# Two linear-attention blocks and two MLP blocks on one core, rewritten on a dependency graph whose order a list scheduler settles

## The chip, the cores and the metric

The kernel runs on one core of a Trainium2 chip, as one launch. The metric is the device time of one execution in microseconds (us), lower being better. Five engines work side by side, each through its own list of instructions in order: TensorE (PE in the profile; PEld is its weight load), VectorE (DVE), ScalarE (ACT), GpSimd (POOL) and SyncE (SP), which here issues DMAs only. They meet through semaphores. PSUM, where matmuls end, has eight banks of 128 x 512 fp32.

## The reference

x has 2048 rows of 512. Four layers follow each other, A, B, A, B, with the same weights both times; each takes a layernorm of x and adds its result to x.

```python
def _A_ref(x, wqkv, wo):                       # called with _layernorm(x); H = 32 heads of 16
    qkv = (x @ wqkv).reshape(B, S, 3, H, Dh)   # -> q, k, v
    phi = lambda t: jnp.where(t > 0, t + 1, jnp.exp(t)) + 1e-6
    pq, pk = phi(q), phi(k)
    kv = jnp.einsum("bhsd,bhse->bhde", pk, v)
    z = jnp.einsum("bhsd->bhd", pk)
    num = jnp.einsum("bhqd,bhde->bhqe", pq, kv)
    den = jnp.einsum("bhqd,bhd->bhq", pq, z)[..., None] + 1e-6
    return (num / den).reshape(B, S, D) @ wo

def _B_ref(x, w1, b1, w2, b2):                 # called with _layernorm(x); F = 1792
    y = _layernorm(x)
    h = gelu_tanh(y @ w1 + b1)
    return h @ w2 + b2
```

kv and z sum over all 2048 rows, so the second half of a layer A can't begin before its first half has ended. Every other step is by rows.

## The kernel before

The rows are cut into 16 tiles of 128 and 4 chunks of 4 tiles. Python writes the order out by hand: each layer is a generator that emits, step by step, the stages of several tiles, each stage some steps behind the one before (A_LAGS, AB_LAGS, B_LAGS). x stays in SBUF as fp32 (`xsb`).

Layer A, first half, by tile: the layernorm (`ln_stats`, L316 to L323: stats, their aggregate and veps on DVE, a power of -1/2 on POOL; L383: the normalized tile in bf16 on DVE), a DMA transpose from the SP queue into `yTA` (L368), then q as 16 matmuls of 128 columns (L429), k (L439) and v (L447) as 4 of 512 each. phi is exp and relu on ACT (L461 to L465), then a minimum and an addition on DVE (L481 to L499). v is copied out of PSUM, in half the tiles by DVE (L472) and in the others by ACT. Per tile 4 matmuls of 128 columns (L515) add to K'V and 4 of 8 columns (L518) to z. At the end DVE masks both to the heads' diagonal blocks (`KVm` L560, `Zm` L562).

Second half, by tile: numerator (L576) and denominator (L578) as 4 matmuls each, the numerator copied to SBUF by ACT (L595), the reciprocal on DVE (L602, L617), the product on POOL (L618), a transpose by 4 matmuls (L645) with its copy by ACT (L649), wo (L668) and the addition to x on DVE (L677).

Layer B, by chunk: the same layernorm, with the normalized tile on ACT (L379), a DMA transpose into `yTB`, w1 in 14 groups of 4 matmuls of 512 columns (L764). The gelu takes five passes over each 128 x 512 group, half of the groups with ACT's square and half with DVE's: ACT L784 and L788, DVE L804, L814, L822, L826, ACT's sigmoid L837, DVE's product L851. w2 is 14 matmuls by tile (L865) and a fifteenth for b2 (L867); L873 adds to x.

A layer's matmuls wait until the layer before has issued all of its own: `prev_pe_done` and `my_pe_done` hold them back, while layernorms may run ahead. At the start SP loads x in four parts of 512 KB, the first of which ACT turns to fp32 (L272); POOL loads wqkv, wo, w1 and w2, one DMA each. At the end ACT makes bf16 of each tile (L1000) and SP stores it.

## Time and profile before

| | before |
|---|---|
| three timed runs | 418.62, 419.04, 420.08 us; median 419.04 |
| span of the profiled execution | 415.4 us, 6985 instructions |
| busy PE, DVE, ACT, POOL | 364.7, 309.6, 316.6, 76.5 us |
| mean granted TensorE clock | 0.978 |

The profiled execution is known by its span, from its first to its last instruction: 415.4 us. The timed runs show 3.6 us more in the median for what lies around the span. A busy time adds up instructions that may overlap (matmuls are pipelined, and the next elementwise instruction starts some 0.1 us before the one ahead has ended), so it is above the time that the engine needs. The granted clock is a share of full speed; TensorE has two levels, 1.2 and 2.4 GHz.

### The profile page before, as it was taken

To read this page: it belongs to the slowest core of one execution; us is meant where nothing else is said; L and a number is where in the kernel's file an instruction comes from. 1 tells how busy PE (TensorE), PEld (TensorE's weight loads), DVE (VectorE), ACT (ScalarE), POOL (GpSimd) and SP (SyncE) were. 2 spreads that over 40 slices of the span, in tenths; PEclk is the share of its full clock that TensorE was granted. 3 is DMA by queue.
4 is the path that set the end of the run, shared out by engine and by line. 5 is a ranking of instruction groups with operands and counts; after the bars stand their busy time and mean duration, and the time that the engine had idled before them with its cause. 6 is when DMAs were issued, how large, how long until landed. Compare 5 with 4: busy or idle time off the path is not lost.

```text
span 415.4 us, 6985 instructions
## 1 busy us (share of the span) xinstructions
PE 364.7 (88%) x2465; PEld 185.4 (45%) x2465; DVE 309.6 (75%) x868; ACT 316.6 (76%) x563; POOL 76.5 (18%) x115
## 2 busy tenths in 40 slices
PE   0869997979967999999999999796996799999986
PEld 0546665544422444445435666553432244444432
...
DMA packets 40448, 18.80 MB, mean 45 GB/s; under 512 B 35229, under 2 KB 39326, under 8 KB 40414
## 3 DMA queue, kind: packets, MB, share of 16 engines
...
## 4 chain that ended last, share of the span: by engine, by line
PE 62%; DVE 19%; ACT 8%; DMA 5%; issue 4%; POOL 1%; ACTq 0%; POOLq 0%
PE ps L865 24%; PE ps L764 19%; PE ps L429 5%; PE ps L439 4%; DVE stats L316 4%; DMA yTA<-ybuf 4%; PE ps L447 4%; DVE xsb L677 3%; ACT ub L784 3%; ACT sgb L837 2%; PE ps L867 2%; PE ps L668 2%; DVE rr L617 2%; DVE mv L317 1%; DVE ybuf L383 1%
## 5 line engine op out<-in xcount | busy, mean ns | idle before, releaser
L764 PE MATMUL ps<-yTB,w 128*128 128x512 bf16 x448 | 103.8, 380 | 9.9 <-ACT qb L788 7.9
L865 PE MATMUL ps<-w,bigB 128*128 128x512 bf16 x448 | 102.1, 379 | 5.5 <-DVE bigB L851 5.5
L784 ACT ACTIVATE ub<-ps,b1c 128x512 bf16<-128x512 f32 x112 | 78.4, 704 | 19.5 <-DVE bigB L851 14.2
L323 POOL TENSOR_TENSOR rstd<-veps,neghalf 128x1 f32<-128x1 f32 x64 | 36.4, 568 | 219.3 <-DVE veps L322 148.3
L837 ACT ACTIVATE sgb<-wb 128x512 bf16<-128x512 bf16 x112 | 72.8, 653 | 3.7 <-DVE wb L822 1.9
L764 PEld LDWEIGHTS ps<-yTB,w 128*128 128x128 bf16 x448 | 40.6, 98 | 68.0 <-ACT qb L788 10.4
L865 PEld LDWEIGHTS ps<-w,bigB 128*128 128x128 bf16 x448 | 42.8, 98 | 58.9 <-DVE bigB L851 7.3
L873 DVE TENSOR_TENSOR xsb<-ps,xsb 128x512 f32<-128x512 f32 x32 | 22.0, 689 | 49.4 <-PE ps L867 49.4
L851 DVE TENSOR_TENSOR bigB<-ub,sgb 128x512 bf16<-128x512 bf16 x112 | 46.8, 419 | 12.2 <-ACT sgb L837 10.9
L316 DVE BATCH_NORM_STATS2 stats<-xsb 128x6 f32<-128x512 f32 x64 | 43.0, 671 | 8.5 <-ACT xsb L272 8.5
L461 ACT ACTIVATE ebq<-ps 128x512 bf16<-128x512 f32 x32 | 19.1, 598 | 38.6 <-PE ps L429 30.3
L429 PE MATMUL ps<-yTA,wqkv 128*128 128x128 bf16 x512 | 35.4, 224 | 12.2 <-DMA yTA<-ybuf 12.2
L618 POOL TENSOR_TENSOR ob<-numb,rr 128x512 bf16<-128x512 f32 x32 | 33.6, 1057 | 38.5 <-DVE rd L602 23.6
L788 ACT ACTIVATE qb<-ps,b1csa 128x512 bf16<-128x512 f32 x56 | 39.5, 706 | 0.0
L822 DVE SCALAR_TENSOR_TENSOR wb<-qb,ub 128x512 bf16<-128x512 bf16 x56 | 38.3, 684 | 0.0
L429 PEld LDWEIGHTS ps<-yTA,wqkv 128*128 128x128 bf16 x512 | 30.6, 100 | 13.7 <-DMA yTA<-ybuf 12.6
L668 PE MATMUL ps<-wo,oT 128*128 128x512 bf16 x128 | 35.0, 401 | 1.6 <-DVE xsb L677 1.6
L439 PE MATMUL ps<-wqkv,yTA 128*128 128x512 bf16 x128 | 34.4, 393 | 0.0
L447 PE MATMUL ps<-wqkv,yTA 128*128 128x512 bf16 x128 | 32.9, 379 | 0.0
L649 ACT ACTIVATE oT<-ps 128x512 bf16<-128x512 bf16 x32 | 19.1, 596 | 14.5 <-PE ps L645 14.4
L804 DVE TENSOR_TENSOR qb<-ub 128x512 bf16<-128x512 bf16 x56 | 23.4, 418 | 4.2 <-ACT ub L784 4.1
L379 ACT ACTIVATE ybuf<-xsb,nmr,rstd 128x512 bf16<-128x512 f32 x32 | 26.2, 819 | 0.0
...
## 6 DMA issues: line engine op xcount, KB each, us to landing
...
yTA<-ybuf SPq DMA_TRANSPOSE x32, 2.5
...
yTB<-ybuf SPq DMA_TRANSPOSE x32, 2.5
b1rows<-in_B_b_dram SPq DMA_DIRECT2D x1, 3.5 KB
```

The costliest lines, as they stand in the source:

```text
L316: t1 = dve.emit(lambda e: e.bn_stats(stats[:, ss, :], src_ap), deps=[x_dep, war_get(("stat", ss))])
L429: ins = e.matmul(ps[:, QBK[qs], kt * P:(kt + 1) * P], lhsT=wqkv_sb[:, dt, kt * P:(kt + 1) * P], rhs=yTA[:, dt, yts * P:(yts + 1) * P], sta ...
L439: ins = e.matmul(ps[:, KBK[qs], :], lhsT=yTA[:, dt, yts * P:(yts + 1) * P], rhs=wqkv_sb[:, dt, D:2 * D], start=(dt == 0), stop=(dt == DT - 1))
L447: ins = e.matmul(ps[:, VBK[qs], :], lhsT=yTA[:, dt, yts * P:(yts + 1) * P], rhs=wqkv_sb[:, dt, 2 * D:3 * D], start=(dt == 0), stop=(dt == ...
L668: ins = e.matmul(ps[:, WOBK[ws], :], lhsT=oT[:, j, ots * P:(ots + 1) * P], rhs=wo_sb[:, j, :], start=(j == 0), stop=(j == DT - 1))
L764: ins = e.matmul(ps[:, hb, :], lhsT=w1_sb[:, dt, ft * P:(ft + 1) * P], rhs=yTB[:, dt, y0 * P:(y0 + 4) * P], start=(dt == 0), stop=(dt == D ...
L784: d["t_u"] = act.emit(lambda e: e.activation(ub[:, us, :], ps[:, hb, :], ACT.Identity, bias=b1c[:, ft:ft + 1], scale=1.0), deps=[d["t_h"], ...
L788: d["t_q2"] = act.emit(lambda e: e.activation(q2b[:, us, :], ps[:, hb, :], ACT.Square, bias=b1csa[:, ft:ft + 1], scale=sa), deps=[d["t_h"] ...
L822: d["t_w"] = dve.emit(lambda e: e.scalar_tensor_tensor(out=wb[:, us, :], in0=q2b[:, us, :], scalar=1.0, in1=ub[:, us, :], op0=ALU.add, op1 ...
L837: d["t_s"] = act.emit(lambda e: e.activation(sgb[:, us, :], wb[:, us, :], ACT.Sigmoid, scale=GELU_2C), deps=[d["t_w"], war_get(("sgb", us))])
L851: t_g = dve.emit(lambda e: e.tensor_tensor(gT[:, gs, ft, :], ub[:, us, :], sgb[:, us, :], op=ALU.mult), deps=[d["t_s"], war_get(("gT", gs, ...
L865: e.matmul(ps[:, 3 + ws, :], lhsT=gT[:, gs, ft, k * P:(k + 1) * P], rhs=w2_sb[:, ft, :], start=(ft == 0), stop=False)
```

## The change

The file is written anew. Each operation is a node (`Op`) with a planned duration, the buffers that it reads and writes, and a priority; `Scheduler.run` plays the plan through and fixes each engine's order, the buffers' slots and the PSUM banks; `assign_waits` then makes the semaphore waits from the graph. In the plan each issuing queue (SP, ACT, POOL) has a transfer time of its own. At run time the lists are fixed, as before.

In the computation: v is no longer formed. Per tile y^T phi(k) is summed (`attn_g_held`: 4 matmuls of 512 columns into four PSUM banks, layer 0; `attn_g_chunk`: by chunk, added up in SBUF by DVE, layer 1), and once per layer multiplied with Wv (`attn_kv`, 16 matmuls of 128 columns). z is summed elementwise on POOL (`zacc`), and four matmuls of one column sum it over partitions. q is formed by chunk with 512 columns. Numerator and denominator are one matmul of 136 columns, times 4. DVE multiplies straight out of PSUM. The transpose ahead of wo is a DMA transpose from SP. The gelu is one ACT instruction from PSUM. b2 is added to x on POOL. x comes into bf16 tiles that the first layernorm reads directly, the last addition writes bf16. Normalized tiles of layer 0's first half are on DVE, later ones on ACT for every second tile.

The order of layers by chunk is new: `attn_out` and the MLP of chunk c, and the first half of the second layer A for that chunk, have priorities 40 us apart by chunk, so they interleave.

```diff
-                        ins = e.matmul(ps[:, VBK[qs], :], lhsT=yTA[:, dt, yts * P:(yts + 1) * P],
-                                       rhs=wqkv_sb[:, dt, 2 * D:3 * D], start=(dt == 0), stop=(dt == DT - 1))
...
+        def attn_g_held(L, st, k, y, ykey, pk, gb, prio):
+            def fn(e):
+                for dc in range(DT):
+                    ins = e.matmul(ps[:, gb.slot + dc, :], lhsT=yb[:, y.slot, dc * P:(dc + 1) * P], rhs=pkb[:, pk.slot, :],
+                                   start=(st == 0), stop=(st == ST - 1))
...
+                G.op("pool", lambda e: e.tensor_tensor(zacc[:], zacc[:], pkb[:, pk.slot, :], op=ALU.add), 1060,
...
+                    ins = e.matmul(v[:, kt, 0:136], lhsT=yTa(pq)[:, kt, k * P:(k + 1) * P],
+                                   rhs=kvz[:, kt_.slot, kt * 136:(kt + 1) * 136], start=True, stop=True)
...
+            def mul(e):
+                return e.tensor_tensor(ob[:, o.slot, :].rearrange("p (k h x) -> p k h x", k=DT, h=8),
+                                       pair(b)[:, :, 0:P].rearrange("p k (h x) -> p k h x", h=8),
+                                       rr[:, r.slot, :].rearrange("p (k h) -> p k h", k=DT).unsqueeze(3).broadcast_to([P, DT, 8, DH]),
+                                       op=ALU.mult)
+            G.op("dve", mul, 680, reads=[f"rr{L}_{st}", f"n{L}_{st}"], writes=[f"o{L}_{st}"], tiles=[b, r, o], prio=prio,
+                 name=f"o{L}_{st}", lat=40)
+            dma("sp", lambda e: e.dma_start_transpose(oT[:, ot.slot, :].rearrange("p (d s) -> p d s", d=DT), ob[:, o.slot, :]),
...
-                    d["t_s"] = act.emit(lambda e: e.activation(sgb[:, us, :], wb[:, us, :], ACT.Sigmoid, scale=GELU_2C),
...
+                G.op("act", lambda e, ft=ft, b=b: e.activation(gT[:, g.slot, ft * 512:(ft + 1) * 512], bank(b), ACT.Gelu_apprx_tanh,
+                                                               bias=b1c[:, ft:ft + 1], scale=1.0),
...
+            G.op("pool", lambda e: e.tensor_tensor(xsb[:, st, :], xsb[:, st, :], b2b[:], op=ALU.add), 1060,
...
+            busy = 1300.0 if transpose else 100.0 + kb * 1024 / 230.0
...
+                begin = max(at + 100.0, dma_free[e])
+                dma_free[e] = begin + o.nbytes
...
+                dma("act", lambda e: e.dma_start(wqkv[:, :, D:2 * D], wsrc[:, :, D:2 * D]), ["wk"], prio=-99.5, name="wk", kb=512)
+        for c in range(1, NC):
+            dma("act", lambda e, c=c: e.dma_start(
...
+                if st == 3:
+                    late("wv", "wv", wqkv[:, :, 2 * D:3 * D], wsrc[:, :, 2 * D:3 * D], pr, 512, [tr])
+                if st == 4:
+                    late("wo", "wo", wo[:], A_wo.rearrange("(dt p) c -> p dt c", p=P), pr, 512, [tr])
+                if st == 5:
+                    consts(pr, [tr])
+                if st in (6, 8):
+                    h = (st - 6) // 2
+                    late(f"w1_{h}", f"w1_{h}", w1[:, 2 * h:2 * h + 2, :], B_w1.rearrange("(dt p) c -> p dt c", p=P)[:, 2 * h:2 * h + 2, :],
+                         pr, 896, [tr])
...
+    P_A2=-30.0, P_W1=0.0, P_W2=54.0, P_K=77.0, P_G=90.0, P_Q=140.0, STEP=4.2,
+    A1_Q=58.7, A1_STEP=1.0, N_H=3, N_N=2, GAP=17.0, TABLE_PENALTY=16.9, WINDOW=199.0,
```

What this makes of the instructions is shown at three places, before and after. The first is POOL in the first half of the first layer A. Before, its list holds the power of each tile (L323) and the weights' loads (L281, L240, L243), and nothing else waits:

```order
L281 DMA wqkv<-in_A_wqkv_dram 128x4x1536
L323 TENSOR_TENSOR rstd<-veps,neghalf 128x1 [waits g_dve] x2
L240 DMA wo<-in_A_wo_dram 128x4x512
L323 TENSOR_TENSOR rstd<-veps,neghalf 128x1 [waits g_dve] x2
L251 MEMSET onesm 128x512
L252 AFFINE_SELECT bdmask<-onesm 128x512 [waits g_pool]
L254 AFFINE_SELECT bdmask<-bdmask 128x512 [waits g_pool]
L256 AFFINE_SELECT hmask<-onesm 128x32
L258 AFFINE_SELECT hmask<-hmask 128x32 [waits g_pool]
L260 AFFINE_SELECT identb<-onesm 128x128
L323 TENSOR_TENSOR rstd<-veps,neghalf 128x1 [waits g_dve] x2
L243 DMA w1<-in_B_w1_dram 128x4x1792
```

In the changed kernel, from the middle of that stage (L488 is the power, L547 the sum of phi(k), L455 a weight's load; d_yT6, d_yT8 and d_yT0 are the landings of the transposes of tiles 6, 8 and 10):

```order
L455 DMA w1<-in_B_w1_dram 128x2x1792 [waits d_yT6]
L547 TENSOR_TENSOR zacc<-zacc,pkb 128x512 [waits g_dve]
L488 TENSOR_TENSOR rstd<-veps,neghalf 128x1
L547 TENSOR_TENSOR zacc<-zacc,pkb 128x512 [waits g_pool,g_dve]
L488 TENSOR_TENSOR rstd<-veps,neghalf 128x1
L547 TENSOR_TENSOR zacc<-zacc,pkb 128x512 [waits g_pool,g_dve]
L488 TENSOR_TENSOR rstd<-veps,neghalf 128x1
L455 DMA w1<-in_B_w1_dram 128x2x1792 [waits d_yT8]
L488 TENSOR_TENSOR rstd<-veps,neghalf 128x1 x3
L488 TENSOR_TENSOR rstd<-veps,neghalf 128x1 [waits g_dve]
L455 DMA w2<-in_B_w2_dram 128x7x512 [waits d_yT0]
L547 TENSOR_TENSOR zacc<-zacc,pkb 128x512 [waits g_dve]
```

The powers of tiles 8 to 14 now stand behind loads that wait for the transposes of tiles 6 and 8 to land; that of tile 15 stands behind one that waits for tile 12, and behind the sums up to tile 11.

The second is PE where the first layer B begins. Before, all 16 tiles of wo (L668, the last rows of them here, with the transposes L645) stand ahead of the first w1 (L764):

```order
L668 MATMUL ps<-wo,oT 128x512 x4
L645 MATMUL ps<-identb,ob 128x128 x4
L668 MATMUL ps<-wo,oT 128x512 x8
L764 MATMUL ps<-yTB,w1 128x512 x96
L865 MATMUL ps<-w2,bigB 128x512 x14
L867 MATMUL ps<-b2row,ones_row 128x512
L764 MATMUL ps<-yTB,w1 128x512 x16
```

In the changed kernel (L650 numerator and denominator, L558 q, L674 wo, L694 w1, L711 w2):

```order
L674 MATMUL ps<-wo,oT 128x512 x8
L650 MATMUL ps<-kvz,t4 128x136 x4
L674 MATMUL ps<-wo,oT 128x512 x4
L650 MATMUL ps<-kvz,t4 128x136 x4
L558 MATMUL ps<-t4,wqkv 128x512 x4
L694 MATMUL ps<-t4,w1 128x512 x4
L650 MATMUL ps<-kvz,t4 128x136 x4
L694 MATMUL ps<-t4,w1 128x512 x44
L674 MATMUL ps<-wo,oT 128x512 x4
L694 MATMUL ps<-t4,w1 128x512 x8
L674 MATMUL ps<-wo,oT 128x512 x12
L650 MATMUL ps<-kvz,t4 128x136 x8
```

The first w1 stands behind four tiles of wo, and the next chunk's wo inside the first chunk's MLP.

The third is PE where the second layer A's sums end. Before, the last w2 of the first layer B (L865, L867) has only tile 0's sums and the next tiles' q, k and v (L429 to L447) behind it:

```order
L865 MATMUL ps<-w2,bigB 128x512 x14
L867 MATMUL ps<-b2row,ones_row 128x512
L515 MATMUL ps<-vb,pkb 128x128
L518 MATMUL ps<-ones8,pkb 128x8
L515 MATMUL ps<-vb,pkb 128x128
L518 MATMUL ps<-ones8,pkb 128x8
L515 MATMUL ps<-vb,pkb 128x128
L518 MATMUL ps<-ones8,pkb 128x8
L515 MATMUL ps<-vb,pkb 128x128
L518 MATMUL ps<-ones8,pkb 128x8
L429 MATMUL ps<-yTA,wqkv 128x128 x16
L439 MATMUL ps<-wqkv,yTA 128x512 x4
```

In the changed kernel (L592 y^T phi(k) of a chunk, L537 k, L616 z, L623 the product with Wv):

```order
L711 MATMUL ps<-w2,gT 128x512 x14
L592 MATMUL ps<-pkb,yb 128x512 x16
L537 MATMUL ps<-wqkv,t4 128x512 x12
L558 MATMUL ps<-t4,wqkv 128x512 x12
L537 MATMUL ps<-wqkv,t4 128x512 x4
L558 MATMUL ps<-t4,wqkv 128x512 x8
L592 MATMUL ps<-pkb,yb 128x512 x8
L616 MATMUL ps<-ones32,zacc 128x1 x4
L592 MATMUL ps<-pkb,yb 128x512 x8
L558 MATMUL ps<-t4,wqkv 128x512 x4
L623 MATMUL ps<-wqkv,gtb 128x128 x16
L558 MATMUL ps<-t4,wqkv 128x512 x4
```

Of the second layer A's first half only the last chunk's sums and eight groups of q are left behind the last w2 here. On DVE the four additions of the chunk before (L602 of the changed kernel) stand between the last tile's stats and their aggregate.

## Rows read from the trace of the kernel before

**Rows 1.** The page, part 1: busy us, share of the span, instructions.

```profile
PE 364.7 (88%) x2465; PEld 185.4 (45%) x2465; DVE 309.6 (75%) x868; ACT 316.6 (76%) x563; POOL 76.5 (18%) x115
```

**Rows 2.** Stretches: us, busy (instructions) by engine, PEclk, DMA share, GB/s.

```profile
0.00:10.00 10.00, 0.19 (x1) 0.10 (x1) 3.43 (x9) 3.68 (x8) 3.64 (x13) 1.00 0.77 258
120.00:130.00 10.00, 6.22 (x24) 1.86 (x24) 9.17 (x28) 10.00 (x19) 1.21 (x2) 1.00 0.07 14
160.00:170.00 10.00, 10.00 (x47) 4.40 (x47) 7.99 (x21) 8.62 (x16) 0.00 (x0) 1.00 0.00 0
270.00:280.00 10.00, 9.35 (x85) 5.63 (x84) 7.40 (x24) 6.12 (x12) 6.54 (x8) 0.79 0.01 2
```

**Rows 3.** The chain that ended last: start us, us, what.

```profile
67.90 0.60 DVE KVm L560
...
101.57 10.38 PE ps L764 x48
...
149.80 3.02 PE ps L865 x14
...
411.92 0.70 DVE xsb L873
412.64 0.63 ACT big L1000
```

**Rows 4.** Instructions by line: busy us, mean ns, idle before and its releasers.

```profile
L764 PE MATMUL ps<-yTB,w 128*128 128x512 bf16 x448 | 103.8, 380 | 9.9 <-ACT qb L788 7.9 <-ACT ub L784 1.4
...
L784 ACT ACTIVATE ub<-ps,b1c 128x512 bf16<-128x512 f32 x112 | 78.4, 704 | 19.5 <-DVE bigB L851 14.2 <-PE ps L764 3.4 <-DVE wb L826 1.8
L837 ACT ACTIVATE sgb<-wb 128x512 bf16<-128x512 bf16 x112 | 72.8, 653 | 3.7 <-DVE wb L822 1.9 <-DVE wb L826 1.7
...
L316 DVE BATCH_NORM_STATS2 stats<-xsb 128x6 f32<-128x512 f32 x64 | 43.0, 671 | 8.5 <-ACT xsb L272 8.5
...
L323 POOL TENSOR_TENSOR rstd<-veps,neghalf 128x1 f32<-128x1 f32 x64 | 36.4, 568 | 219.3 <-DVE veps L322 148.3 <-DVE veps L319 71.0
...
L618 POOL TENSOR_TENSOR ob<-numb,rr 128x512 bf16<-128x512 f32 x32 | 33.6, 1057 | 38.5 <-DVE rd L602 23.6 <-DVE rr L617 8.8 <-ACT numb L595 3.8
...
L677 DVE TENSOR_TENSOR xsb<-ps,xsb 128x512 f32<-128x512 f32 x32 | 21.6, 682 | 5.4 <-PE ps L668 5.4
...
L461 ACT ACTIVATE ebq<-ps 128x512 bf16<-128x512 f32 x32 | 19.1, 598 | 38.6 <-PE ps L429 30.3 <-DVE big L484 8.0
...
L383 DVE TENSOR_SCALAR ybuf<-xsb,mv,rstd 128x512 bf16<-128x512 f32 x32 | 17.5, 546 | 2.7 <-POOL rstd L323 2.7
...
L499 DVE TENSOR_TENSOR pkb<-ebk,rbk 128x512 bf16<-128x512 bf16 x32 | 13.6, 426 | 1.6 <-ACT rbk L465 0.5
...
L317 DVE BATCH_NORM_AGGREGATE mv<-stats 128x2 f32<-128x6 f32 x64 | 11.6, 182 | 2.2
...
L617 DVE RECIPROCAL rr<-rd 128x32 f32<-128x32 f32 x32 | 11.3, 353 | 3.6 <-POOL ob L618 2.7
...
L496 DVE TENSOR_SCALAR ebk<-ebk 128x512 bf16<-128x512 bf16 x32 | 9.1, 284 | 0.7 <-ACT ebk L464 0.7
...
L560 DVE TENSOR_TENSOR KVm<-ps,bdmask 128x512 bf16<-128x512 f32 x2 | 1.4, 684 | 0.0
```

**Rows 5.** The transposes into yTA, whole span: ns min/median/max; landing in us.

```profile
L368 SPq DMA_TRANSPOSE yTA<-ybuf x32: 1189/1191/2015, 7.4 to 255.9; - x32
...
DMA to landing us min/median/max: 2.4/2.5/8.3
```

**Rows 6.** The transpose issued between 23 and 24.5 us, beside the load of w1.

```profile
DMA to landing us min/median/max: 8.3/8.3/8.3
```

**Rows 7.** The transpose issued between 37 and 39 us, beside the load of w2.

```profile
DMA to landing us min/median/max: 3.9/3.9/3.9
```

**Rows 8.** DVE, then POOL, from 13.4 us: start us, us, instruction.

```profile
13.53 0.72 DVE L383 TENSOR_SCALAR ybuf<-xsb,mv,rstd 128x512 bf16<-128x512 f32 x1 [0.66 <-POOL rstd L323]
...
14.05 0.91 POOL L252 TENSOR_SCALAR_AFFINE_SELECT bdmask<-onesm 128x512 bf16<-128x512 bf16 x1
```

More of the change, by code (lines that the diff above doesn't have):

```diff
@@ L11 @@
 P = 128
+S = 2048
 D = 512
@@ new lines, with __init__, op @@
+class Graph:
+    def __init__(self):
+        self.ops = []
+        self.writer = {}
+        self.readers = {}
+        self.parts = {"w1": ("w1_0", "w1_1"), "w2": ("w2_0", "w2_1")}
+    def op(self, eng, fn, dur, reads=(), writes=(), tiles=(), prio=0.0, name="", lat=0.0, table=None, sem=None,
+           nbytes=0, after=()):
+        o = Op(eng, fn, dur, lat, prio, name, table, sem, nbytes)
+        o.seq = len(self.ops)
+        reads = [p for k in reads for p in self.parts.get(k, (k,))]
+        for k in reads:
+            w = self.writer.get(k)
+            assert w is not None, f"{name} reads {k} before it is written"
+            o.deps[w] = True
+        for k in writes:
+            w = self.writer.get(k)
+            if w is not None:
+                o.deps[w] = True
+            for r in self.readers.get(k, ()):
+                o.deps[r] = True
+        for k in reads:
+            self.readers.setdefault(k, []).append(o)
+        for k in writes:
+            self.writer[k] = o
+            self.readers[k] = []
+        for a in after:
+            o.deps[a] = True
+        o.deps.pop(o, None)
+        for t in tiles:
+            if t not in o.tiles:
+                o.tiles.append(t)
+                t.users += 1
+        self.ops.append(o)
+        return o
@@ new lines, with __init__, options, when @@
+class Banks:
+    def __init__(self, classes):
+        self.name = "psum"
+        self.classes = classes
+        self.state = [(0.0, ()) for _ in range(8)]
+        self.held = {c: 0 for c in classes}
+    def options(self, t):
+        allowed, cap = self.classes[t.cls]
+        if self.held[t.cls] >= cap:
+            return
+        for b in allowed:
+            span = range(b, b + t.width)
+            if all(self.state[i] is not None for i in span):
+                yield max(self.state[i][0] for i in span), b
+    def when(self, t):
+        return min((o[0] for o in self.options(t)), default=None)
+    def take(self, t):
+        _, b = min(self.options(t))
+        users = []
+        for i in range(b, b + t.width):
+            users += self.state[i][1]
+            self.state[i] = None
+        self.held[t.cls] += 1
+        t.slot = b
+        return users
+    def give(self, t, at):
+        self.held[t.cls] -= 1
+        for i in range(t.slot, t.slot + t.width):
+            self.state[i] = (at, tuple(t.done))
```

1430 lines of the change are left out of this document (572 added, 858 removed), and 5 rows, old and new, of the table psum.

## The prediction, written before the changed kernel ran

> **What bounds the kernel now.** I read the busy times first [rows 1]: PE 364.7 us of the span of 415.4, DVE 309.6, ACT 316.6. No engine is full, so I looked at stretches [rows 2]. From 160 to 170 us PE is full (10.00 of 10) at full clock, with DVE at 7.99 and ACT at 8.62: there matmuls bound. From 120 to 130 ACT is full and PE has 6.22: the gelu bounds, since layer B's first groups wait for ACT (9.9 us of idle time before L764, most of it for ACT's square) [rows 4]. At 0 to 10 DMA moves 258 GB/s and PE has nothing.
>
> The chain gives two lengths that I need [rows 3]: K'V is masked at 67.90, and the first w1 begins at 101.57, when all 16 tiles of the second half are through. It also gives prices: 48 matmuls of 512 columns in 10.38 us are 0.216 each, and w2's 14 in 3.02 are 0.216 too. Columns set that price, so I take 0.057 for 136 columns and 0.054 for 128 as estimates by columns.
>
> **PE, part by part.** Per tile and layer A the change drops K'V and z (4 x 136 columns) and the transposes (512), per tile of layer B the b2 matmul (512): 32 x 1568 columns = 50,176, at 0.216 per 512 that is 21 us. y^T phi(k) costs what v cost. What is left: 1408 matmuls of 512 columns, 304.1 us; 128 of 136 columns, 7.3; 32 of 128 columns, 1.7: 313 us. The old span minus 334 is some 80 us in which PE did not stream; most of the change's worth must come from there.
>
> **The other engines under it.** In layer 0 a chunk holds 112 matmuls of the MLP, 48 of k, q and y^T phi(k), 16 of wo: 176 x 0.216 + 0.9 = 39 us of PE. DVE per tile there, with [rows 4] (0.68 for each PSUM operation after L677 and L560, 0.18 for each tiny one): den, reciprocal and product 1.21; two additions to x 1.36; two stats with aggregates and veps 2.06; normalizing 0.7; phi of k and q 4 passes, 1.42: 6.75, and a chunk's sums 4 x 0.68: 29.7 us. ACT: 14 gelus, 16 passes for phi at 0.6, four norms at about 0.8, two table loads: 25 us. POOL: 8 powers at 0.57 and 8 additions at 1.06 (nearest row L618): 13 us. All three stay below 39, so in the middle PE should stream.
>
> The gelu's own price is in no row. The nearest from below is exp at 0.598, from above Identity with a bias at 0.704 [rows 4]. I take 0.70, since it too reads PSUM with a bias; a group of w1 costs PE 0.864, so at either end it is hidden. If it is not (two passes, 0.70 + 0.65), a chunk's 14 groups take 18.9 instead of 12.1 us.
>
> **First half of layer 0.** Bytes are as before, and 3 MB (x, Wk, Wq) are asked for at once on three queues. By the measured 258 GB/s they land by about 12 us, and the transposes of tiles 0 to 4, issued from about 5.5 us on, land between 10 and 14.5. Then POOL's list sets the pace: its loads wait for transposes to land, and powers stand behind them. Leg by leg, with 1.06 per sum, 0.57 per power, about 1 per issue and 1.2 per transpose issued [rows 4, 5]: tile 4 lands 14.5; two sums, the load of wo, the masks (2.7) and half of w1 later, and after the transposes of tiles 5 and 6, tile 8's power ends at 28.2; its transpose is issued at 28.8 beside that load and lands at 33; the other half of w1 goes out at 34, tiles 11 and 12 are issued at 35 to 36 and land at 41 to 42; the second half of w2 and the sum of tile 11 let tile 15's power end at 45.6; it lands at 50.0. A transpose beside a load took 8.3 us for w1 and 3.9 for w2 [rows 6, 7], 2.5 alone [rows 5]; I used 4.2, 6 and 3.8, as half of w1 is in flight a shorter time. K, exp and relu, phi, y^T phi(k), copies, product with Wv and mask add 0.9 + 1.2 + 0.7 + 0.9 + 1.3 + 0.9 + 0.7 plus handovers: **57** (before: 68.5). With all transposes at 2.5 it is 51, with all at 8.3 it is 68. DVE's own work there is about 38 us, PE's 35: neither is last.
>
> The Trainium skill, "DMA: Bandwidth & Descriptors", section "Issuing engines are not separate DMA queues", says that DMAs from several engines run on the same 16 DMA engines and interleave. It speaks against the plan's transfer time per queue; the 258 GB/s at the start, with SP and POOL both loading, agrees. By the plan's 230 GB/s on each queue the first transposes would land some 5 us sooner, and the sum would be about 358 instead of 363.
>
> **From the mask to the first w1.** Numerators 0.5; on DVE four times 1.21, four times addition, stats, aggregate and veps (1.71), and 1.4 for two normalizations and the fifth tile's reciprocal ahead of the last one; power 0.57, normalization 0.55, transpose 2.5: **17** us, before 33. The transposes of o (2.5 instead of PE's transpose and a copy) are hidden here, since DVE has four products to do before the first addition. PE has 7 groups of q, 7 numerators and four tiles of wo meanwhile, 11 us.
>
> **From there PE counts.** First w1 at 74. Up to the last w2 of layer 1 the list holds 608 matmuls of 512 columns and 36 of 136: 133.4, so 207.4. Then the second layer A closes: the last addition and stats 1.4; four sums of the chunk before, which DVE has ahead of the aggregate, until 4.6; power, normalization and transpose until 8.6; k, phi and y^T phi(k) until 15.4; last sum, product and mask until 18; with handovers 18.6, and 17 more to the next w1: **35.6**, of which PE's list fills 24. So 243.0. The last part holds 496 and 28: 108.7, so 351.7. The tail is addition, store and landing: before, 412.64 less 411.92 plus what follows ACT's copy [rows 3], 415.4 - 411.92 - 0.63 = 2.9: 354.6. After PE's idle time before, the granted clock was 0.79 of 2.4 GHz over 10 us [rows 2], so part of them ran at the 1.2 GHz level and 2.1 us were lost; twice that: 358.8. One us for small waits (0 to the 9.9 that L764 had): 359.8 of span. The profiled execution of before lies 3.6 below the median of its runs; with as much around it the time is **363**.
>
> **Rivals.**
> - *Smoother than I think*: transposes land at 2.5 throughout (51), and clock and small waits cost nothing: 363 - 6 - 5 = 352. For it: PE, DVE and ACT have slack. Against it: the load of weights did stretch transposes [rows 6].
> - *POOL and DVE hold each other up*: 64 POOL passes over 128 x 512 are new. A normalization beside POOL's mask took 0.72 instead of 0.546 [rows 8, 4]. If every such pass shuts out DVE, a chunk needs 29.7 + 8.5 = 38.2, still within PE's 39, but the two ways from mask to w1 grow by 4 additions each (4.2), and the first half by about 4: 375. The Trainium skill, "SBUF — State Buffer", section "Who interferes with whom", calls the port pair of DVE and GpSimd an exclusive lock; the 0.18 us above is far less than a whole POOL pass, so the row bears out only a part of it.
> - *The gelu is not one pass*: 6.8 us per chunk, eight chunks: 363 + 54 = 417, about as before. Nothing in the trace shows the function.
> - *Slower than before*: every chunk's way from numerator to w1 lies open, because the engines' lists are fixed and a late transpose holds all behind it on SP, DVE and PE. The open way is 17 - 11 = 6 us; with its two transposes halfway between 2.5 and 8.3 [rows 5, 6] it is 11.8, in six more chunks 71: 434. It decides from 9.3 us per chunk on. Against it: w2 and w1 of the neighbour chunk (24 us of PE) stand between, and no weights are loaded any more.
>
> **How the numbers follow.** The forecast has a chance of 0.65, smoother 0.15, the port 0.15, gelu 0.02, slower 0.03. The range takes in smoother with both ways from mask to w1 2 us shorter (348), and the port with the first half some 6 later (381). A difference of 0.3% is about what a measurement of this kernel can tell from none. Faster 0.95, same 0.02, slower 0.03.
>
> **What would show it.** In the new profile: the mask of layer 0 near 57, first w1 near 74 and that of the last layer near 243; PE full, at full clock, for most of 80 to 205 and 245 to 352; POOL's powers of tiles 8, 11 and 15 right behind landings; gelu at 0.6 to 0.7; ACT below 200 us. A mask before 52, or PE below 9 of 10 in the middle, would prove me wrong.

## The result, and the profile after

The changed kernel takes 372.35 us (median of four runs, 372.08 to 372.79), the kernel before on the same chip 418.83: a ratio of 0.888, 95% interval 0.884 to 0.892. That is faster, inside the range, and 9.35 us above the forecast of 363.0. The profiled execution has a span of 370.5, 1.85 us below the median. Ratios below are taken from fast runs; one run of b1 (405.0 us) was in a slower state and is not in its ratio.

Page part 1 of after, busy us by engine, then the stretches that answer to [rows 2] (us, busy us by engine in the order PE, PEld, DVE, ACT, POOL, granted clock, share of the DMA engines, GB/s):

```profile
PE 328.2 (89%) x1585; PEld 148.7 (40%) x1585; DVE 234.0 (63%) x566; ACT 172.5 (47%) x275; POOL 117.6 (32%) x148
```

```profile
0.00:10.00 10.00, 0.00 (x0) 0.00 (x0) 3.17 (x9) 1.28 (x1) 2.65 (x11) 1.00 0.83 258
20.00:40.00 20.00, 17.50 (x77) 6.84 (x78) 19.03 (x55) 11.02 (x22) 16.44 (x23) 1.00 0.49 133
120.00:130.00 10.00, 10.00 (x53) 4.76 (x52) 8.01 (x20) 4.42 (x6) 3.87 (x5) 1.00 0.18 37
160.00:170.00 10.00, 10.00 (x48) 4.51 (x46) 8.64 (x18) 7.09 (x12) 4.38 (x5) 1.00 0.13 26
250.00:260.00 10.00, 4.68 (x18) 1.74 (x16) 8.18 (x24) 3.04 (x4) 3.81 (x5) 0.56 0.40 81
```

From 120 to 130 us ScalarE was full before and TensorE had 6.22; now TensorE is full and ScalarE has 4.42. In the first half (20 to 40) VectorE is the full engine, 19.03 of 20. From 250 to 260 the granted clock is 0.56: it fell to 0.50, which is the 1.2 GHz level, at about 251, after TensorE had been busy for 0.42 of the 4 us before 252, and was back at 1.00 by 262.

The groups that answer to [rows 4] (busy us, mean ns, idle before):

```profile
L700 ACT ACTIVATE gT<-ps,b1c 128x512 bf16<-128x512 f32 x112 | 75.9, 686 | 48.5 <-PE ps L694 48.2
L685 POOL TENSOR_TENSOR xsb<-xsb,b2b 128x512 f32<-128x512 f32 x32 | 37.3, 1168 | 23.7 <-ACT yb L495 13.4
L547 POOL TENSOR_TENSOR zacc<-zacc,pkb 128x512 f32<-128x512 f32 x30 | 35.0, 1168 | 15.4 <-DVE pkb L526 13.7
```

The gelu is one pass of 686 ns (forecast 0.70). GpSimd's additions take 1168 ns instead of the 1.06 that I took from L618.

Five places divide the run: the first numerator (L650), the first w1 (L694), the last w2 of the first layer (L711), the w1 of the last layer, and the end of its last w2. TensorE's timeline of after at four of them (start us, us, instruction, idle before and its releaser):

```profile
63.75 0.65 PE L650 MATMUL ps<-kvz,t 128*128 128x136 bf16 x8
...
82.30 1.79 PE L694 MATMUL ps<-t,w 128*128 128x512 bf16 x4 [0.63 <-ACT rb L522]
...
215.62 3.19 PE L711 MATMUL ps<-w,gT 128*128 128x512 bf16 x14
...
256.14 6.17 PE L694 MATMUL ps<-t,w 128*128 128x512 bf16 x16 [2.58 <-DMA t<-yb]
```

The chain of after, at the boundary to the last layer (start us, us, what), which answers to [rows 3]:

```profile
246.81 1.16 POOL xsb L685
...
249.14 1.15 POOL xsb L685
...
256.14 13.08 PE ps L694 x48
```

Two additions of b2 stand in it, and the first 48 matmuls of the last part take 13.08 us, where 48 took 10.38 before.

The five places in the kernels of the experiments that start from the changed kernel, read in the same way (us from the start, then the stretches in between; the letter and number is that of the experiment). Each row is one execution, the profiled one; f3's was the slowest of its four (375.34 us, median 372.72):

| kernel | first numerator | to first w1 | to last w2 | boundary to w1 | to the end |
|---|---|---|---|---|---|
| forecast | 57 | 17 | 133.4 | 35.6 | 108.7 |
| after | 63.75 | 18.55 | 136.51 | 37.33 | 111.42 |
| e1, weights' loads free of waits | 65.92 | 18.78 | 136.50 | 37.34 | 111.22 |
| e2, z sums on one column | 61.21 | 19.18 | 135.83 | 36.39 | 111.10 |
| e3, b2 on one column | 63.92 | 17.99 | 135.56 | 37.01 | 111.32 |
| e4, both | 61.90 | 18.09 | 133.99 | 36.05 | 111.33 |
| e5, first loads in one queue | 65.56 | 18.93 | 136.52 | 37.27 | 111.11 |
| f1, w1 and w2 loaded late | 60.58 | 27.69 | 137.02 | 37.89 | 111.35 |
| f3, matmuls in the idle time | 64.10 | 19.22 | 137.86 | 40.52 | 108.99 |
| g1, w2 late | 61.68 | 25.79 | 137.19 | 37.61 | 109.89 |
| g2, w2 and b2 late | 61.97 | 25.38 | 138.78 | 37.10 | 110.82 |
| g3, second layer A not beside layer B | 63.84 | 18.83 | 112.92 | 67.15 | 111.31 |
| h1, loads spread by need | 62.07 | 18.52 | 136.52 | 37.17 | 111.35 |

### The profile page after: what moved, and what is told of

Its sections match the earlier page's. It is cut to its first block, busy times and chain, and to the rows that moved or that the text cites. A ratio compares the mean times of both kernels' runs of the same rounds, so it can differ in the third digit from the quotient of the medians.

```text
span 370.5 us, 4473 instructions
## 1 busy us (share of the span) xinstructions
PE 328.2 (89%) x1585; PEld 148.7 (40%) x1585; DVE 234.0 (63%) x566; ACT 172.5 (47%) x275; POOL 117.6 (32%) x148
## 3 DMA queue, kind: packets, MB, share of 16 engines
q1 hardware_dynamic: 55276, 15.35, 19.8%
## 4 chain that ended last, share of the span: by engine, by line
PE 67%; DVE 17%; DMA 6%; issue 4%; ACT 3%; POOL 3%; SPq 0%; DVEq 0%; ACTq 0%
PE ps L694 26%; PE ps L711 22%; DMA t<-yb 5%; PE ps L674 5%; PE ps L537 4%; PE ps L592 4%; PE ps L558 3%; DVE stats L477 3%; DVE yb L500 3%; DVE eb L524 2%; DVE pkb L526 2%; DVE ob L662 2%; ACT eb L520 2%; POOL rstd L488 1%; POOL xsb L685 1%
## 5 line engine op out<-in xcount | busy, mean ns | idle before, releaser
L694 PE MATMUL ps<-t,w 128*128 128x512 bf16 x448 | 102.3, 388 | 3.3 <-DMA t<-yb 2.6
L711 PE MATMUL ps<-w,gT 128*128 128x512 bf16 x448 | 100.5, 380 | 0.0
L700 ACT ACTIVATE gT<-ps,b1c 128x512 bf16<-128x512 f32 x112 | 75.9, 686 | 48.5 <-PE ps L694 48.2
L488 POOL TENSOR_TENSOR rstd<-veps,neghalf 128x1 f32<-128x1 f32 x64 | 35.7, 561 | 170.0 <-DVE veps L482 114.4
L694 PEld LDWEIGHTS ps<-t,w 128*128 128x128 bf16 x448 | 44.2, 99 | 59.3 <-issue 3.9
L520 ACT ACTIVATE eb<-ps 128x512 bf16<-128x512 f32 x64 | 38.6, 605 | 55.6 <-PE ps L537 33.7
L711 PEld LDWEIGHTS ps<-w,gT 128*128 128x128 bf16 x448 | 43.4, 98 | 50.2
L685 POOL TENSOR_TENSOR xsb<-xsb,b2b 128x512 f32<-128x512 f32 x32 | 37.3, 1168 | 23.7 <-ACT yb L495 13.4
L522 ACT ACTIVATE rb<-ps 128x512 bf16<-128x512 f32 x64 | 38.5, 607 | 7.3 <-PE ps L537 4.1
L547 POOL TENSOR_TENSOR zacc<-zacc,pkb 128x512 f32<-128x512 f32 x30 | 35.0, 1168 | 15.4 <-DVE pkb L526 13.7
L537 PE MATMUL ps<-wqkv,t 128*128 128x512 bf16 x128 | 33.8, 406 | 6.8 <-DMA t<-yb 6.8
L674 PE MATMUL ps<-wo,oT 128*128 128x512 bf16 x128 | 31.2, 380 | 3.9 <-DVE xsb L678 1.3
L558 PE MATMUL ps<-t,wqkv 128*128 128x512 bf16 x128 | 32.4, 388 | 0.0
L524 DVE TENSOR_SCALAR eb<-eb 128x512 bf16<-128x512 bf16 x64 | 23.9, 374 | 11.8 <-ACT eb L520 11.6
L537 PEld LDWEIGHTS ps<-wqkv,t 128*128 128x128 bf16 x128 | 12.6, 103 | 25.0 <-issue 6.8
L526 DVE TENSOR_TENSOR pkb<-eb,rb 128x512 bf16<-128x512 bf16 x32 | 21.6, 676 | 1.5 <-ACT rb L522 0.9
```

The costliest lines, as they stand in the source:

```text
L488: G.op("pool", lambda e: e.tensor_tensor(rstd[:, s.slot:s.slot + 1], veps[:, s.slot:s.slot + 1], neghalf[:], op=ALU.pow), 570, reads=[k + ...
L520: G.op("act", lambda e: e.activation(eb[:, et.slot, :], bank(bt), ACT.Exp), 500, reads=[src_key], writes=[f"e{tag}"], tiles=[bt, et], prio ...
L522: G.op("act", lambda e: e.activation(rb[:, rt.slot, :], bank(bt), ACT.Relu), 500, reads=[src_key], writes=[f"r{tag}"], tiles=[bt, rt], pri ...
L537: ins = e.matmul(bank(b), lhsT=yTa(yT)[:, dt, k * P:(k + 1) * P], rhs=wqkv[:, dt, D:2 * D], start=(dt == 0), stop=(dt == DT - 1))
L547: G.op("pool", lambda e: e.tensor_tensor(zacc[:], zacc[:], pkb[:, pk.slot, :], op=ALU.add), 1060, reads=[f"pk{L}_{st}", "zacc"], writes=[" ...
L558: ins = e.matmul(bank(b), lhsT=wqkv[:, dt, kt * P:(kt + 1) * P], rhs=yTa(yT)[:, dt, :], start=(dt == 0), stop=(dt == DT - 1))
```

## Experiments

Ratios are to the kernel before, measured beside each on the same chip (its medians were 418.8 to 420.4); "against after" is the difference to 0.8876, times 419 us. The interval of a ratio is worth 1.2 to 3.5 us either way: those of e1, e3, e5, f3 and, just, h1 overlap with that of the changed kernel (0.884 to 0.892).

### GpSimd's list and GpSimd's passes

The theory: GpSimd's list, which stands at landings with z sums and powers behind it, paces the first half. The rival: its passes over 128 x 512 hold VectorE up. e1 moves the six loads of weights to ScalarE's list and takes their waits away; the z sums and powers keep their order. e2, e3 and e4 shorten the passes and leave the order as it is. The code is cut to the lines that matter, here and below.

```diff
+        for o in [o for o in order["pool"] if o.name in ("wv", "wo", "w1_0", "w1_1", "w2_0", "w2_1")]:
+            tr = next(d for d in o.deps if d.sem is not None)
+            del o.deps[tr]
...
+            order["act"].insert(next(i for i, a in enumerate(order["act"]) if a.start > o.start), o)
```

> The six loads of wv, wo, w1 and w2 are issued from ScalarE's queue where the plan had them in time, and wait for no transpose; GpSimd's list keeps its arithmetic only. Theory A (GpSimd's list, which stands at landings of transposes while z sums and powers wait behind it, paces the first half of layer 0, the +6.8 us before the first numerator): the first numerator comes 4 to 7 us earlier than 63.8, the whole run takes 366 to 368.5. Theory B (the first half is paced by the first loads and by passes of GpSimd that lock VectorE out): the first numerator moves by less than 1.5 us, the run takes 371 to 373. Theory C (unhindered loads run beside the transposes and stretch them): the first numerator comes later, 373 to 377.

```diff
-                G.op("pool", lambda e: e.tensor_tensor(zacc[:], zacc[:], pkb[:, pk.slot, :], op=ALU.add), 1060,
+                G.op("pool", lambda e: e.tensor_tensor(zacc[:, 0:1], zacc[:, 0:1], pkb[:, pk.slot, 0:1], op=ALU.add), 1060,
```

> The 30 additions into the z sums work on one column instead of 512 (this leaves most of the denominators' sums out); order and every wait are as in the changed kernel. Theory A (GpSimd's passes cost VectorE time at the memory they share, in the attention stretches): VectorE's phi additions fall from 576 to 676 ns to about 430 ns, the first numerator comes 2 to 4 us earlier, the run takes 366 to 369. Theory B (VectorE has slack there, the passes cost nothing in the end): below 1 us, 371.5 to 373.

```diff
-            G.op("pool", lambda e: e.tensor_tensor(xsb[:, st, :], xsb[:, st, :], b2b[:], op=ALU.add), 1060,
+            G.op("pool", lambda e: e.tensor_tensor(xsb[:, st, 0:1], xsb[:, st, 0:1], b2b[:, 0:1], op=ALU.add), 1060,
```

> The 32 additions of b2 work on one column instead of 512 (this leaves most of b2 out); order and every wait are as in the changed kernel. Theory A (a b2 addition of 1.15 us stands on GpSimd ahead of the next tile's power in the chain from the mask to the first w1, twice in each layer, so some 2 us a layer, and the rest of the passes stretch VectorE): the stretch from the first numerator to the first w1 falls from 18.5 to 16.5 us in layer 0, the run takes 367 to 369.5. Theory B (the power would have waited for its own statistics anyway): below 1 us, 371.5 to 373.

> Both of the former at once: z sums and b2 additions on one column (this leaves most of both out). If GpSimd's passes are what the prediction missed: the two gains add up to 5 to 8 us, 364 to 367, and VectorE's busy time falls from 234 to about 215 us. If both stretches are limited by something else (first loads, clock, TensorE's order): 370 to 372, although VectorE's time falls the same.

Measured: e1 374.57 us, 0.892 (0.888 to 0.896), 1.8 against after; e2 368.2, 0.877 (0.873 to 0.881), -4.4; e3 369.94, 0.882 (0.879 to 0.885), -2.3; e4 366.37, 0.873 (0.871 to 0.876), -6.0. The waits of GpSimd's list at landings are not what paces the first half: freed of them it gained nothing, and the numerator came 2.2 us later. The transposes in the chain (start us, us, what), of after, then of e1, show why:

```profile
6.48 6.92 DMA t<-yb
...
17.58 3.94 DMA t<-yb
...
38.70 5.74 DMA t<-yb
```

```profile
6.87 6.67 DMA t<-yb
...
17.72 4.83 DMA t<-yb
...
35.61 6.34 DMA t<-yb
...
46.15 6.43 DMA t<-yb
```

The loads, no longer held back, ran beside more transposes. That was theory C of e1.

What e1 left in place is the order of the list. In both kernels tile 15's power stands behind the z sum of tile 11; its statistics are ready at 37.7 us in after and at 37.9 in e1. GpSimd of after, then of e1:

```profile
52.72 0.74 POOL L488 TENSOR_TENSOR rstd<-veps,neghalf 128x1 f32<-128x1 f32 x1
```

```profile
54.08 0.73 POOL L488 TENSOR_TENSOR rstd<-veps,neghalf 128x1 f32<-128x1 f32 x1
```

In after VectorE, busy without a gap, comes to that tile's normalization at 53.62, 0.15 us behind the power's end. So the two lists arrive there together, and whether the power's place alone costs anything is open: no kernel here moves it ahead of the sums.

The passes, in contrast, cost 6.0 us. e2 and e4 fell where their expectations had them; e3's 369.94 lies between its two theories, and its way to the first w1 fell by 0.56 us, not by 2. VectorE's groups of after, then of e4:

```profile
L477 DVE BATCH_NORM_STATS2 stats<-xsb 128x6 f32<-128x512 f32 x48 | 33.2, 692 | 1.1
...
L524 DVE TENSOR_SCALAR eb<-eb 128x512 bf16<-128x512 bf16 x64 | 23.9, 374 | 11.8 <-ACT eb L520 11.6
...
L526 DVE TENSOR_TENSOR pkb<-eb,rb 128x512 bf16<-128x512 bf16 x32 | 21.6, 676 | 1.5 <-ACT rb L522 0.9
...
L526 DVE TENSOR_TENSOR t<-eb,rb 128x512 bf16<-128x512 bf16 x32 | 18.4, 576 | 1.9 <-ACT rb L522 1.2
...
L500 DVE TENSOR_SCALAR yb<-xsb,mv,rstd 128x512 bf16<-128x512 f32 x24 | 15.8, 657 | 3.3 <-POOL rstd L488 2.7
```

```profile
L477 DVE BATCH_NORM_STATS2 stats<-xsb 128x6 f32<-128x512 f32 x48 | 33.2, 692 | 1.1
...
L524 DVE TENSOR_SCALAR eb<-eb 128x512 bf16<-128x512 bf16 x64 | 19.4, 305 | 18.2 <-ACT eb L520 18.0
...
L526 DVE TENSOR_TENSOR t<-eb,rb 128x512 bf16<-128x512 bf16 x32 | 13.6, 425 | 2.6 <-ACT rb L522 1.9
L526 DVE TENSOR_TENSOR pkb<-eb,rb 128x512 bf16<-128x512 bf16 x32 | 13.5, 422 | 3.1 <-ACT rb L522 2.8
L500 DVE TENSOR_SCALAR yb<-xsb,mv,rstd 128x512 bf16<-128x512 f32 x24 | 13.0, 540 | 2.5 <-POOL rstd L488 1.9
```

Three kinds of pass lose their surplus (L524 4.5, L526 8.1 and 4.8, L500 2.8 us, and 1.4 in L500's second form), the statistics none. Of these 21.6 us at most 6 reached the end: shorter passes also free GpSimd for the powers behind them, which these runs do not separate. By the table they come off the first half (1.85), the stretch in which TensorE is full (2.5), the boundary (1.3) and the way to the first w1 (0.5).

### One part alone: the gelu

```diff
-                    d["t_u"] = act.emit(lambda e: e.activation(ub[:, us, :], ps[:, hb, :], ACT.Identity, bias=b1c[:, ft:ft + 1], scale=1.0),
...
+                t_g = act.emit(lambda e: e.activation(gTs(sc % 3, ft), ps[:, hb, :], ACT.Gelu_apprx_tanh,
+                                                      bias=b1c[:, ft:ft + 1], scale=1.0),
```

> The kernel before, with its seven-step gelu replaced by one activation from PSUM with the bias, and three gelu buffers instead of two; PE's order and all of layer A stay. Theory A (the gelu bounded only single stretches, since TensorE bounds layer B otherwise; most of the change's 46 us comes from the attention, its TensorE columns and the overlap): 400 to 410, ScalarE's busy time falls by about 80 us, VectorE's by about 60, and L764's 9.9 us of idle time ahead go below 2. Theory B (the gelu was the main part): below 390. Theory C (it was hidden): 417 to 420.

401.52 us, 0.952 (0.944 to 0.960): 20 of the 47 us (17 to 24 by the interval), theory A. The third buffer for the gelu's output is in it. Its busy line and its w1:

```profile
PE 356.9 (90%) x2422; PEld 187.5 (47%) x2465; DVE 187.8 (47%) x532; ACT 227.9 (58%) x391; POOL 75.4 (19%) x115
```

```profile
L768 PE MATMUL ps<-yTB,w 128*128 128x512 bf16 x438 | 99.3, 379 | 0.7 <-issue 0.3
```

ScalarE lost 89 us and VectorE 122 (I had said about 60: the squares, products and the last multiplication of 112 groups are gone, several passes each). L764's 9.9 us of idle time [rows 4] are 0.7 here. With the gelu in one pass TensorE has hardly a wait left before w1. What the change gains beyond these 20 us I put down to columns of TensorE and to overlap; only the overlap has a run of its own (g3).

### Where the loads lie, and the clock

> The changed kernel, the four loads of w1 and w2 (3.6 MB) issued only behind the last transpose of the first half of layer 0, on GpSimd's queue after the last z sum but one; nothing else moves. Theory A (these loads stretch the transposes beside them, and GpSimd's waits on landings come with them): the landings of the transposes fall to 2.5 to 3.5 us from tile 5 on, the first numerator comes 4 to 7 us earlier than 63.8, the whole takes 365 to 369; w1 lands by 70, ahead of its first use. Theory B (the first half is paced by VectorE and GpSimd's passes and by the first loads): first numerator 62.5 to 64, 371 to 373.

> The changed kernel, the first loads (x of all tiles, Wk, Wq) in one queue, ScalarE's, in the order in which they are needed, instead of three queues at once. Theory A (x's first tile shares the DMA engines with Wk and with Wq, which is wanted 40 us later; its landing at 5.42 and the first transpose of 6.92 us come from that): tile 0 lands at about 4, the first K product starts 2 to 4 us earlier, the first numerator 1 to 3 us earlier, 369 to 371. Theory B (one queue moves less than three, or the gain is eaten by the weights behind): no gain or up to 3 us lost, 372 to 376.

> The changed kernel with 26 matmuls of 512 columns more, whose results nobody reads, placed where TensorE stands idle ahead of the first w1 of layer 0 (9) and of the last layer (17). Theory A (the granted clock of 0.56 in 250 to 260 comes of the idle time ahead and costs the last part 2.7 us and the first w1 some 1 us): L694's first 48 matmuls of the last part fall from 13.08 to about 10.4 us, the whole takes 368.5 to 370.5. Theory B (the level doesn't come back by this, or the added matmuls push the chain as far as the clock gains): 371.5 to 374.

The edits, one after the other: f1, the four loads behind the next to last z sum; e5, the nine first loads at the head of ScalarE's list; f3, matmuls into a free bank.

```diff
+        last = named["TA0_15"]
+        at = order["pool"].index(named["z0_15"]) + 1
+        for n in ("w1_0", "w1_1", "w2_0", "w2_1"):
...
+            order["pool"].insert(at - 1, o)
+            o.deps = {last: True}
...
+        first = [next(o for o in G.ops if o.name == n) for n in ("x0", "wk", "x1", "x2", "x3", "xc1", "wq", "xc2", "xc3")]
...
+        order["act"][0:0] = first
...
+            w = Op("pe", lambda e, b=b, n=n: [e.matmul(ps[:, b, :], lhsT=wqkv[:, 0, 0:P], rhs=wqkv[:, 0, 0:D], start=True, stop=True)
+                                             for _ in range(n)][-1], n * MM, 0.0, first.prio, "warm" + before)
```

f1: 377.84 us, 0.898 (0.892 to 0.904), 4.4 against after. Half of theory A came true: the first numerator is 3.2 us earlier, with tile 10's transpose landing after 2.4 us instead of the 5.74 in the chain of after. f1 takes away the loads and GpSimd's waits for them together; as e1 took away the waits and gained nothing, I put the 3.2 down to the loads. But the way to the first w1 grew by 9.1. The landings of the first 16 transposes in f1 (min, median, max us), and of the four transposes of o issued from 62 us on:

```profile
DMA to landing us min/median/max: 2.4/2.4/7.0
```

```profile
L668 SPq DMA_TRANSPOSE oT<-ob x4: 1190/1266/3010, 62.4 to 72.5; - x4
...
DMA to landing us min/median/max: 2.4/8.0/9.3
```

The loads now ran beside the transposes of o. I had asked when w1 is needed, not what runs while it lands. e5: 373.54 us, 0.889 (0.883 to 0.894), no gain, theory B; the first product of k starts at 15.38 instead of 13.45, because in one queue x's second tile landed behind Wk, at 8.2 us instead of 5.4 (the 5.42 that I had called the first tile's was the second's), and tile 0's normalization stands behind its statistics on VectorE.

f3: 372.72 us, 0.887 (0.881 to 0.894), no difference that this interval of 2.7 us either way can show. TensorE's timeline of f3 (L835 are the added matmuls), to be held against the last row of the timeline of after above:

```profile
256.16 2.74 PE L835 MATMUL ps<-wqkv 128*128 128x512 bf16 x6 [2.74 <-DVE ob L662]
258.69 0.66 PE L650 MATMUL ps<-kvz,t 128*128 128x136 bf16 x4
259.14 2.77 PE L835 MATMUL ps<-wqkv 128*128 128x512 bf16 x6
261.70 4.59 PE L694 MATMUL ps<-t,w 128*128 128x512 bf16 x20
```

In after w1 begins with 0.39 us a matmul (6.17 for 16), in f3 with 0.23 (4.59 for 20), and the last part shrinks from 111.4 to 109.0: the clock's cost is real. But the added matmuls ran at 0.46 each and waited for a bank until VectorE had read it, so in this execution the w1 came 3.2 us later. Both theories were half right, and in the median the sum is nothing.

### Later loads of w2, later b2, no overlap

> The changed kernel with the two loads of w2 alone moved, from beside the transposes of the first half to a place on GpSimd's queue behind the powers of the first four tiles of layer B, where the transposes of chunk 0 are all issued or landed; w1 stays where it was. Theory A (a load is hidden only where no transpose that somebody waits for runs beside it; f1_late_w lost at the transposes of o what it gained before): the landings of the last transposes of the first half fall to 2.4 us, the first numerator comes at 61 to 62.5, the stretch from there to the first w1 stays at 18 to 19, the whole takes 369.5 to 371.5. Theory B (w2 now comes too late for its first use, or meets the next chunk's transposes): first w2 later than 45 us behind the first numerator, 373 to 378.

> The same, and each chunk's four additions of b2 moved on GpSimd behind the chunk's last power; everything is computed. Theory A (two additions of 1.15 us stand ahead of powers in each of the two open chains): from the first numerator to the first w1 16 to 17 us, the boundary 35 to 36, 366.5 to 369.5. Theory B (GpSimd's passes cost through the memory that they share with VectorE, wherever they stand): no more than 0.7 us below g1_w2_late.

> The changed kernel, planned with k, y^T phi(k) and q of the second layer A due only behind all of layer B of the first layer, so that almost none of them runs beside it (45 of its 48 groups of matmuls come behind the last w2 group but one). Theory A (the overlap is the main part: VectorE has some 4.1 us a tile there, 66 us for 16 tiles, which hides under TensorE's 136 us of the first layer B): the stretch between the last w2 and the w1 of the last layer grows by 50 to 60 us, that of layer B shrinks by 30 to 36, the whole takes 388 to 400. Theory B (TensorE's columns set the time in either order): 372 to 378.

The edits, one after the other: g1, the two loads of w2 behind the power of tile 3 of layer B; g2, besides that, each chunk's b2 additions behind its last power; g3, the second layer A's products planned last.

```diff
+        for n in ("w2_0", "w2_1"):
...
+            order["pool"].insert(order["pool"].index(named["powB0_3"]) + 1, o)
...
+                        p.insert(p.index(last) + 1 + sum(names[f"b2{L}_{4 * c + m}"] in p[p.index(last):] for m in range(k)), o)
...
-    P_A2=-30.0, P_W1=0.0, P_W2=54.0, P_K=77.0, P_G=90.0, P_Q=140.0, STEP=4.2,
+    P_A2=-30.0, P_W1=0.0, P_W2=54.0, P_K=1077.0, P_G=1090.0, P_Q=1140.0, STEP=4.2,
```

g1: 378.54 us, 0.901 (0.894 to 0.908), 5.7 against after. The numerator is 2.1 us earlier as expected; then the last of the four transposes ahead of the first w1, issued 1.5 us behind the loads, stands in the chain:

```profile
77.63 9.76 DMA t<-yb
```

I had misread the plan: the power of tile 3 is ahead of its transpose by a normalization and SP's 1.2 us. g2: 379.36, 0.904 (0.896 to 0.911), theory B. Between the two profiled executions, moving b2 behind the powers won 0.4 and 0.5 us in the two open chains and lost 1.6 in the middle; the medians differ by 0.8 us, less than either interval. Behind the power in question VectorE has work of its own that ends no sooner: in after its timeline from 64.20 to 77.07 has gaps of 0.37 us and less. So the two b2 additions that the chain of after names there are worth some half a us, not the 2 us that I expected.

g2 shows best how VectorE waits, since four b2 additions run in a row. GpSimd, then VectorE, in g2:

```profile
78.44 4.91 POOL L685 TENSOR_TENSOR xsb<-xsb,b2b 128x512 f32<-128x512 f32 x4
```

```profile
78.58 1.32 DVE L526 TENSOR_TENSOR t<-eb,rb 128x512 bf16<-128x512 bf16 x1
79.82 1.24 DVE L524 TENSOR_SCALAR eb<-eb 128x512 bf16<-128x512 bf16 x1
81.10 1.25 DVE L526 TENSOR_TENSOR t<-eb,rb 128x512 bf16<-128x512 bf16 x1
82.27 1.24 DVE L524 TENSOR_SCALAR eb<-eb 128x512 bf16<-128x512 bf16 x1
83.55 0.43 DVE L526 TENSOR_TENSOR t<-eb,rb 128x512 bf16<-128x512 bf16 x1
83.89 0.29 DVE L524 TENSOR_SCALAR eb<-eb 128x512 bf16<-128x512 bf16 x1
```

While GpSimd adds, each phi pass of VectorE takes 1.24 to 1.32 us, as long as a pass of GpSimd; at 83.55, with GpSimd through, 0.43 and 0.29. In after, beside the same addition, an addition from PSUM and the statistics are not touched:

```profile
73.29 0.68 DVE L678 TENSOR_TENSOR xsb<-ps,t 128x512 f32<-128x512 f32 x1
74.00 0.69 DVE L477 BATCH_NORM_STATS2 stats<-xsb 128x6 f32<-128x512 f32 x1
```

```profile
73.23 1.15 POOL L685 TENSOR_TENSOR xsb<-xsb,b2b 128x512 f32<-128x512 f32 x1 [1.19 <-ACT yb L495]
```

The Trainium skill, "SBUF — State Buffer", section "Who interferes with whom", says that a VectorE instruction with two inputs in SBUF contends with a GpSimd instruction that reads SBUF, and that one with at most one input in SBUF, outside the two-port modes, does not. It adds that in a two-port mode whichever of the two issues first has the shared ports for its whole instruction while the other is blocked. The rows agree for the phi products of L526 (two inputs in SBUF), the statistics and the addition from PSUM (one each); for L524, with one input, the trace doesn't show the mode, and its 1.24 us fit the two-port case alone.

g3: 379.69 us, 0.903 (0.896 to 0.910), 6.4 against after. The stretch of layer B shrinks by 23.6 and the boundary grows by 29.8, so running the second layer A beside layer B is worth some 6 us, not the 16 to 28 that I expected; the time lies just above theory B's 378. Stretch 200 to 260 of after, then of g3:

```profile
200.00:260.00 60.00, 49.14 (x254) 22.78 (x252) 49.94 (x121) 25.85 (x47) 18.81 (x21) 0.93 0.18 36
```

```profile
200.00:260.00 60.00, 48.17 (x236) 21.51 (x238) 54.01 (x116) 33.53 (x62) 22.51 (x22) 0.90 0.14 29
```

Left alone, the second layer A still keeps TensorE busy for 48.17 of 60 us: VectorE (54.01) keeps up better than the 4.1 us a tile that I had counted for it.

### The loads spread by need

```diff
+        move("wq", "pool", "powA0_4")
+        move("xc3", "act", "b1c")
+        move("xc2", "act", "b1c")
+        move("w2_1", "pool", "b20_3", "TB0_3")
+        move("w2_0", "pool", "b20_3", "TB0_3")
```

> The changed kernel with its loads spread by the time at which they are needed, all else as planned: Wq issued behind the fifth power instead of first, x's tiles 8 to 15 behind the copy of b1, and w2 behind the landing of the transpose of tile 3 of layer B (g1_w2_late had it 3 us earlier, on top of that transpose). Theory A (a load costs what the transposes beside it lose, at the start and ahead of the mask alike, and costs nothing where no one waits for a transpose): the first product of k starts at 10 to 12 instead of 13.45, the first numerator comes at 59 to 62 instead of 63.8, from there to the first w1 18 to 19.5, the whole takes 366.5 to 370.5. Theory B (VectorE, with GpSimd's passes on top, paces the first half whatever the loads do): the first numerator at 62.5 to 64, 371 to 373. Theory C (the moved loads meet other transposes): a landing above 5 us ahead of the first w1, 374 to 380.

369.69 us (six runs, 369.3 to 370.43), 0.881 (0.877 to 0.885), 2.9 against after; the runs of the two don't overlap, the intervals of the ratios do by 0.001, so a gain is likely and about 0.7%. It is the fastest kernel here that computes everything. The moves at the start did little at first: the first product of k starts at 9.21 instead of 13.45, but the second waits until 14.73 for a transpose that takes 6.15 us, with Wq and x's last tiles now under way at that time, and the fourth ends at 20.0 (19.8 in after). Yet tile 10's transpose, in the chain of h1, is 0.85 us ahead of the one in the chain of after (38.70), before after issues any load of w2 (44.73):

```profile
37.85 5.71 DMA t<-yb
```

In e3, f1, f3, g1, g2 and g3, whose start is that of after, it is issued at 38.8 to 39.3. So about half of the numerator's 1.7 us seems to come from the start and the rest from w2, now behind the landing of the last transpose; no run separates the two. This time the gain was kept to the end.

## Why the prediction was right, and where its sum was off

Sign, size and the binding engine were right; the stretches sum to 15.9 us more than forecast, against the 5.2 that I had set aside for clock and small waits, so the span is 10.7 above 359.8. Beyond it there were 1.85 us instead of 3.6, which leaves 8.95; the sum of 363.4 had been put down as 363, which makes 9.35. The 3.6 was mis-read: in every run with a span on record the time is 1.7 to 1.8 us above its own span, so some 1.9 of the 3.6 will have been that the profiled execution of before was shorter than the median. All five stretches ran over, so no error hid another, but the time lies nearer to the 375 of the port than to the forecast.

- **TensorE's columns.** From the first w1 to the last w2 of layer 1 the forecast was 133.4; e4, without GpSimd's passes, has 133.99. The count of columns holds to 0.6 us, and the 2.5 us more of after are the passes.
- **Where the worth comes from.** I wrote that most of it must come from TensorE's time without streaming. By my own count that time fell from 81 us to 57.5 (370.5 less 313), so it was about half: 21 us of columns, 20 by the gelu alone (b1), some 6 by the overlap (g3); these three are measured or counted apart, and nothing here shows that they add.
- **The first half, 57 against 63.75,** was the worst term. I let GpSimd's list and its waits set the pace; e1 took the waits away and gained nothing, and the list's order was not tested. Leg by leg the delay is there from the start: tile 4 lands at 21.5 (forecast 14.5), tile 8's power ends at 33.5 (28.2), tiles 11 and 12 land at 44.9 and 45.4 (41 to 42), and tile 15's power, behind the sum of tile 11 as forecast, ends at 53.5 (45.6). Tile 4's power ended at 13.7, but VectorE's list has tile 0's phi pass, waiting for ScalarE, ahead of tile 4's normalization:

```profile
16.00 0.29 DVE L524 TENSOR_SCALAR eb<-eb 128x512 bf16<-128x512 bf16 x1 [2.90 <-ACT eb L520]
...
17.14 0.41 DVE L500 TENSOR_SCALAR yb<-t,mv,rstd 128x512 bf16<-128x512 bf16 x1
```

What the runs can price: transposes beside the loads of w1 and w2 (3.2 us by f1) and GpSimd's passes (1.85 by e4). Both meet a VectorE that is full there (19.03 of 20), and the first transpose took 6.92 us beside the first loads. I had said that VectorE is not last: its own work is what I counted (37.9 us up to 62 in e4, forecast 38), but with GpSimd's passes beside it, it is busy for 46.5 of the first 64 us of after. The 1.7 us left have no experiment; e4 and f1 were not run together.
- **From the mask to w1, 17 against 18.55, and the boundary, 35.6 against 37.33.** The passes are 0.5 and 1.3 of it. I left out that SP issues the transposes of tiles 2 and 3 one after the other, 1.2 us each; no run tests what that costs.
- **The rival of the port** had 0.15 and 375, 12 us above the forecast; by e4 GpSimd's passes cost 6 us, and the rows of g2 show VectorE waiting for whole passes. The step that failed is the sentence on [rows 8]: I read a normalization of 0.72 us beside GpSimd's mask as a loss of 0.18, and took the lock for partial. GpSimd's mask began 0.52 us after the normalization did, and what ran beside it until then was a memset (13.45, 0.52 us), so that row could not show a wait for a whole pass. For the middle the rival added nothing, as I argued that VectorE's 38.2 stay under TensorE's 39; the passes cost 2.5 us there, the largest part, and a mean over a chunk hides that single phi passes stand in the chain (one of 1.34 us at 172.17).
- **The clock.** The last part is 2.7 us above forecast; its first 48 matmuls took 13.08 us against 10.38 [rows 3]. The 4.2 set aside for the clock cover that.
- **The others.** Gelu 686 ns; ScalarE 172.5 (below 200); no late transpose in the middle: the 26 into t issued between 90 and 215 us landed within 2.4 to 2.8 us, and TensorE has 10.00 of 10 from 120 to 130 and 160 to 170.

The account of the 15.9: passes 6.2 (the spans of after and e4), loads beside transposes 3.2 (f1), clock 2.7, and, if these add up, 3.8 in small pieces that no run separates.
